# Windowed attention and two MLPs on one core: most raw weight loads issued from GpSimd's DMA queue in place of SyncE's

## The chip, the cores and the metric

The kernel runs on one core of one Trainium2 chip. The metric is the device time of one execution in microseconds (us), the median of several runs. Engines are named as in the profile: PE (TensorE matmuls), PEld (its weight loads), DVE (VectorE), ACT (ScalarE), POOL (GpSimd), SP (SyncE, which here does nothing but issue transfers). A queue of an engine is marked with a q, so SPq is SyncE's instruction queue.

## The reference

Attention over 4 batches and 8 heads of 576 positions with head size 64, where each position sees itself and the 63 before it; its output, 2304 tokens by 512, goes through two MLPs one after the other:

```
scores = q k^T / 8, masked to 0 <= i - j < 64;  attn = softmax(scores) v
h = x @ w_in;   g = s * max(h, 0)^2 + b;                     x = g @ w_out     (layer one, "moe")
h = x @ w_in2;  g = max(h, 0) + alpha * min(h, 0);           out = g @ w_out2  (layer two, "moe2")
```

Each weight matrix is 512 x 2048 or 2048 x 512 in float32; the kernel gets the weights as 64-bit words, 4096 bytes in each of 128 rows for a block of 128 hidden units.

## The kernel before

The hidden dimension of each layer is cut into 16 blocks of 128 units, called f. Layer one takes the blocks in groups of 3, 3, 4, 2 and 4, layer two in four groups of 4. The first two groups of layer one run beside the attention, token block by token block ("the first part of layer one"; up to about 230 us). From then on each group runs over three token spans of 768 in turn. In this second part two blocks f are handled as a pair by a scheme with seven products in place of eight (`hidden_pair`): PE multiplies seven pieces of x with seven pieces of the weights into the tiles `h` and `ab`, ACT copies partial sums between those (line 956), and then both layers' nonlinearity runs on ACT and DVE; `project` multiplies with w_out into `y`. Every float32 operand is split in a high and a low part, and each product is three matmuls.

Weights arrive raw. `converted` makes one step that loads 512 KB of raw words into a tile `raw` (line 640; a ring of three buffers), two ACT steps that read them (lines 644 and 648), and three DVE steps (653/654, 658, 663). After line 663 the raw buffer is free. There are 64 such loads, 32 of w_in and 32 of w_out. The conversion result `wt` is split into high and low parts (lines 670, 672 and 675; 708 and 711 for w_out of layer one). For w_in in the second part, sums of two blocks are formed first, the pieces are written into a staging ring `ag`, stored to HBM (`wd`, line 758) and loaded again from there before they are used (`aw`, line 779). The pieces of x are likewise stored in `xd` (793, 828) and loaded for each span and group (`ax`, line 911). For w_out of layer one, POOL adds the converted block to `wsum` (line 705), from which a bias is made.

All of this is recorded as steps in a `Plan`, and `Plan.emit` writes the instructions out in an order that it finds by list scheduling: each step names the engines that could do it with a cost and a tail after it, a due time `at` and an earliest time `after`. These numbers set only the order in each engine's queue. On the chip each engine takes its queue strictly in order, and waits at an instruction until the semaphores it needs are there. Before the change every transfer stood in SP's queue; POOL's queue held masks, softmax scaling (line 557), sums of x pieces (843) and the `wsum` additions. A raw load is a step for SP at cost `nbytes / 380e3` (1.4) with a tail of 2.0; its due time is that of the conversion less 8, and its earliest time 30 before that.

Of the kernel before, what the change touches and what calls it, by code (L numbers as in the profile page):

```python
# [18 lines left out]
P = 128  # L19
# [18 lines left out]
GRING = 10  # L38
LAG = 1.7
SOON = 16.0  # L40
PAIR_AT = (0, 3584)
W_AT = (0, 1024, 2048, 3584, 4608, 5632)

# [187 lines left out]
def tile_window_attention_two_mlps(  # L231
# [14 lines left out]
    nc = tc.nc  # L246
# [28 lines left out]
    T = Plan()  # L275
# [25 lines left out]
    def act(cols, fn):  # L301
        return ("act", 0.2 + cols * 0.00084, fn, 0.0)

    def dve(cols, fn, fast=False, port=False):
        return ("dve", 0.15 + cols * (0.00053 if fast else 0.00106), fn, 0.0) + (True,) * (fast or port)
# [4 lines left out]
    def dma(n, nbytes, fn):  # L310
        return [("sp", max(n * 0.45, nbytes / 380e3), fn, 2.0)]
# [24 lines left out]
    with tc.manual_schedule():  # L336
# [293 lines left out]
        def converted(layer, f, part, at, after):  # L630

            key = f"w.{layer}.{f}.{part}"
            src = ((w_in1, w_out1), (w_in2, w_out2))[layer][part][f].bitcast(I32)
            raw = T.tile("raw" + key, wst, [P, 512, 2], I32, "raw", 3)
            t = T.tile("t" + key, wst, [P, 512], F32, "wt", 3)
            L = lambda: T[raw][:, :, 0]
            H = lambda: T[raw][:, :, 1]
            ti = lambda: T[t].bitcast(I32)
            T.step(
                dma(1, P * 4096, lambda: nc.sync.dma_start(out=T[raw].rearrange("p a b -> p (a b)"), in_=src)),  # L640
                writes=[(raw, 0), (raw, 1)], at=at - 8, after=after - 8,
            )
            T.step(
                [act(512, lambda: nc.scalar.activation(T[t], H().bitcast(F32), AF.Abs, scale=65536.0))],  # L644
                reads=[(raw, 1)], writes=[t], at=at, after=after,
            )
            T.step(
                [act(512, lambda: nc.scalar.activation(L(), L().bitcast(U32), AF.Copy, scale=2.0 ** -29))],  # L648
                writes=[(raw, 0)], at=at, after=after,
            )  # L650

            def exponent():
                nc.vector.tensor_scalar(T[t], T[t], W_MIN, W_MAX, op0=ALU.max, op1=ALU.min)
                nc.vector.tensor_scalar(ti(), ti(), 3, None, op0=ALU.logical_shift_left)

            T.step([("dve", 0.8, exponent, 0.0, True)], writes=[t], at=at, after=after)
            T.step(
                [dve(512, lambda: nc.vector.scalar_tensor_tensor(  # L658
                    out=L(), in0=H(), scalar=-0x80000000, in1=L(), op0=ALU.bitwise_and, op1=ALU.bitwise_or), port=True)],
                reads=[(raw, 1)], writes=[(raw, 0)], at=at, after=after,  # L660
            )
            T.step(
                [dve(512, lambda: nc.vector.tensor_tensor(ti(), ti(), L(), op=ALU.add), port=True)],  # L663
                reads=[(raw, 0)], writes=[t], at=at, after=after,
            )
            return t
# [20 lines left out]
        def weight(layer, f, part, at, after):  # L687
            t = converted(layer, f, part, at, after)
            key = f"w.{layer}.{f}.{part}"
            slot = (layer * NF + f) % W_SLOTS[part]  # L690
            if part == 0:
                hi = T.place(key + "h", AW, W_AT[slot], 512, F32R)
                lo = T.place(key + "l", AW, W_AT[slot] + 512, 512, F32R)
            else:
                hi = T.tile(key + "h", wts, [P, 512], F32R, f"woh{slot}")
                lo = T.tile(key + "l", wts, [P, 512], F32R, f"wol{slot}")
            if (layer, part) != (0, 1):
                pair(512, lambda: T[t], lambda: T[hi], lambda: T[lo], [t], [key], at, after)
                return

            def total():
                if f == 0:
                    nc.gpsimd.tensor_copy(wsum, T[t])
                else:
                    nc.gpsimd.tensor_add(wsum, wsum, T[t])

            T.step([pool(512, total)], reads=[t], writes=["wsum"], at=at, after=after)
            T.step([act(512, lambda: nc.scalar.activation(T[hi], T[t], AF.Identity, scale=s_sb[:, 0:1]))],
                   reads=[t, "s"], writes=[hi], at=at, after=after)
            T.step(  # L710
                [dve(512, lambda: nc.vector.scalar_tensor_tensor(
                    out=T[lo], in0=T[t], scalar=s_sb[:, 0:1], in1=f32(T[hi]), op0=ALU.mult, op1=ALU.subtract), port=True)],
                reads=[t, hi, "s"], writes=[lo], at=at, after=after,
            )
# [11 lines left out]
        def weight_pair(n, layer, f1, f2, at, after, direct):  # L726


            ts = [converted(layer, f, 0, at, after) for f in (f1, f2)]
            sums_ = T.place(f"s.{n}", AS, 2 * NMAX, 4 * W2)  # L730
            a = lambda i, j: T[ts[i]][:, j * W2:(j + 1) * W2]
# [36 lines left out]
        def w_slot(n, k):  # L768
            lo, hi = PIECES[k]
            return T.place(f"W{k}.{n}", AW, PAIR_AT[n % 2] + 2 * lo * W2, 2 * (hi - lo) * W2, F32R)  # L770

# [98 lines left out]
        def x_pieces(q, at):  # L870


            t1, t2 = 2 * q * HALF, (2 * q + 1) * HALF
            AYv = AY.rearrange("p (k t) -> p k t", k=NK)
            B = lambda r, c: AYv[:, 2 * r:2 * r + 2, (t1, t2)[c]:(t1, t2)[c] + HALF]
            src = lambda r, c: [f"yh{k}.0.{2 * q + c}" for k in (2 * r, 2 * r + 1)]
            temps = {}

            def add(name, a, b, reads):
                t = T.place(f"T{name}.{q}", AS, name % 2 * C, C)  # L880
                temps[name] = t
                T.step(
                    [dve(C, lambda: nc.vector.tensor_sub(x2(T[t]), a(), b()), port=True)], reads=reads, writes=[t], at=at,
                )

            def piece(j, s, reads):
                x_stage(1, q, j, s, reads, at + ORDER.index(j) * PAIR / 7)

            tv = lambda n: (lambda: x2(T[temps[n]]))
            piece(1, lambda: B(0, 0), src(0, 0))  # L890
            add(1, lambda: B(0, 1), lambda: B(0, 0), src(0, 0) + src(0, 1))
            piece(5, tv(1), [temps[1]])
            add(2, lambda: B(1, 1), tv(1), src(1, 1) + [temps[1]])
            piece(6, tv(2), [temps[2]])
            piece(2, lambda: B(1, 0), src(1, 0))
            add(3, lambda: B(1, 1), lambda: B(0, 1), src(1, 1) + src(0, 1))
            piece(7, tv(3), [temps[3]])
            piece(3, lambda: B(1, 1), src(1, 1))
            add(4, lambda: B(1, 0), tv(2), src(1, 0) + [temps[2]])
            piece(4, tv(4), [temps[4]])  # L900
# [16 lines left out]
        def hidden_pair(layer, g, q, p):  # L917
# [5 lines left out]
            if p == 0 and x_load.held != (layer, q):  # L923
                x_load.held = (layer, q)
                if (layer, g) == (1, 0):
                    x_pieces(q, begin[1, 0, q] - SOON)
                for j in ORDER if (layer, g) != (1, 0) else ():
# [290 lines left out]
        for bi in range(NB):  # L1218
            for hp in range(0, NHP, 2 if bi == 0 else 1):
# [7 lines left out]
                before, after = group(hp // 2 if bi == 0 else bi * NHP + hp, bi, (hp, hp + 1) if bi == 0 else (hp,), at1, at2)  # L1227
# [15 lines left out]
        for g in range(SPLIT[0]):  # L1243
            for i, f in enumerate(groups[0][g]):
                for part in range(2):
                    at = FIRST_W[2 * i + part] if g == 0 else begin[0, g, 0] + (i + 2 * part) * pace[g, 0] - 12.0
# [23 lines left out]
        for x, (layer, g) in enumerate(order_of):  # L1270
# [3 lines left out]
            for p in range(len(fs) // 2):  # L1274
                n = number[layer, g, p]
                at = t + p * PAIR
# [5 lines left out]
            for i, f in enumerate(fs):  # L1282
                at = t + LAG * PAIR + i * PAIR / 4 - 12.0 - 15.0 * end
# [77 lines left out]
```

## Time and profile before

| | |
|---|---|
| median of 3 runs | 852.15 us (851.51 to 853.44) |
| profiled execution, own time | 854.11 us |
| its span, first to last instruction | 852.3 us |
| PE busy | 832.7 us (98%) |
| DVE, ACT, POOL busy | 651.1 (76%), 510.5 (60%), 103.5 us (12%) |
| granted TensorE clock, mean | 0.995 |
| DMA | 202.57 MB, mean 238 GB/s |
| raw loads on SPq | 64, of 512 KB |

Busy times add up what an engine did; an instruction that only issues a transfer is not counted. A wait is the idle time just before an instruction, put down to the engine or transfer whose signal came last. "To landing" is the time from the issue of a transfer to its completion signal.

### The profile page before, as it was taken

The page shows a single profiled execution, that of the slowest core. Times are in us where ns is not written, and L with a number is a line of the kernel's source. Part 1 is how long each engine was busy: PE and PEld are TensorE (multiplying, and loading weights), DVE is VectorE, ACT ScalarE, POOL GpSimd, SP SyncE. Part 2 cuts the span into 40 slices and gives each one's busy share as a digit, 9 for nine tenths or more (in the row PEclk, how much of TensorE's full clock was granted, in tenths as well). Part 3 has the DMA queues.
Part 4 walks back from the last instruction along what each step waited for, and adds up shares of the span by engine and source line. Part 5 has one row for each costly group of instructions (what it writes and reads, how often), then busy time and mean ns, then how long its engine had stood idle before and what let it go on. Part 6 is the DMA issues. An engine that isn't in the chain of part 4 may idle for free.

```text
span 852.3 us, 14883 instructions
## 1 busy us (share of the span) xinstructions
PE 832.7 (98%) x5556; PEld 787.7 (92%) x5556; DVE 651.1 (76%) x1175; ACT 510.5 (60%) x1217; POOL 103.5 (12%) x113
## 2 busy tenths in 40 slices
PE   7799999999999999999999999999999999999997
PEld 4678788888899999899999999999999999999997
DVE  6878799797997794699588989867767975864554
ACT  6878997545676474466365667655554754543431
POOL 6543344432100010011000000000000000000000
PEclk9999999999999999999999999999999999999999
DMA  8676973567578979957689359629774769435822
GB/s 282 195 214 179 297 229 111 209 218 275 202 253 316 406 243 363 380 189 305 225 319 340 131 214 354 239 75 346 259 252 156 243 254 348 144 110 187 295 76 75
DMA packets 65592, 202.57 MB, mean 238 GB/s; under 512 B 6640, under 2 KB 25072, under 8 KB 65520
## 3 DMA queue, kind: packets, MB, share of 16 engines
q1 hardware_dynamic: 65520, 201.62, 66.5%
q8 instruction: 44, 0.72, 0.3%
q14 instruction: 28, 0.23, 0.1%
HBM read 143.66 MB, written 57.93 MB: 237 GB/s over the span
## 4 chain that ended last, share of the span: by engine, by line
PE 88%; DMA 5%; ACT 2%; POOL 2%; DVE 1%; issue 1%; SPq 0%; DVEq 0%; POOLq 0%; ACTq 0%
PE y L1158 38%; PE h L945 18%; PE ab L945 13%; PE h L1075 9%; PE y L1135 4%; PE y L605 2%; DMA wd<-ag 2%; DMA raw<-w_out 2%; PE y L574 2%; PE ab L500 1%; DMA raw<-w_in 1%; POOL as__89 L557 1%; ACT as__89 L539 1%; PE ab L1158 0%; PE h L1158 0%
## 5 line engine op out<-in xcount | busy, mean ns | idle before, releaser
L1158 PE MATMUL y<-ax,woh 128*128 128x384 f32 x1216 | 275.4, 334 | 0.4 <-DVE ay L1207 0.4
L1158 PEld LDWEIGHTS y<-ax,woh 128*128 128x128 f32 x1216 | 216.3, 188 | 1.2 <-DVE ay L1207 0.9
L945 PE MATMUL h<-ax,aw 128*128 128x384 f32 x936 | 185.3, 335 | 0.3 <-ACT r L1022 0.2
L1158 PE MATMUL y<-ax,wol 128*128 128x384 f32 x608 | 169.4, 334 | 0.0
L945 PEld LDWEIGHTS h<-ax,aw 128*128 128x128 f32 x936 | 164.2, 188 | 1.4 <-ACT r L1022 0.6
L945 PE MATMUL ab<-ax,aw 128*128 128x384 f32 x702 | 140.4, 335 | 2.0 <-ACT h L956 1.5
L945 PEld LDWEIGHTS ab<-ax,aw 128*128 128x128 f32 x702 | 123.1, 188 | 2.9 <-ACT h L956 1.8
L1158 PEld LDWEIGHTS y<-ax,wol 128*128 128x128 f32 x608 | 111.1, 188 | 0.0
L1015 DVE TENSOR_TENSOR ax<-r,ax 128x384 fp32r<-128x384 f32 x156 | 86.2, 559 | 9.6 <-ACT ax L1010 7.5
L1207 DVE TENSOR_TENSOR ay<-y,ay 128x384 f32<-128x384 f32 x116 | 60.3, 552 | 38.5 <-PE y L1158 38.4
L1075 PE MATMUL h<-ax,aw 128*128 128x512 f32 (+1 forms) x360 | 85.1, 380 | 0.8 <-DVE ax L623 0.6
L1075 PEld LDWEIGHTS h<-ax,aw 128*128 128x128 f32 x360 | 62.8, 192 | 12.9 <-DVE ax L623 1.0
L1045 DVE SCALAR_TENSOR_TENSOR r<-aq,nalpha,r 128x384 f32<-128x384 f32 x96 | 58.5, 613 | 19.6 <-ACT aq L1042 16.6
L644 ACT ACTIVATE wt<-raw 128x512 f32<-128x512 f32 x64 | 43.3, 678 | 37.1 <-DMA raw<-w_out 16.3
L973 DVE TENSOR_TENSOR aq<-ab,aq 128x768 f32<-128x768 f32 x39 | 37.3, 956 | 31.1 <-PE ab L945 29.1
L1010 ACT CAST ax<-r 128x384 fp32r<-128x384 f32 x83 | 42.6, 514 | 25.9 <-DVE r L1045 23.7
L1041 ACT ACTIVATE r<-aq 128x384 f32<-128x384 f32 x48 | 24.8, 517 | 45.8 <-DVE aq L973 45.8
L658 DVE SCALAR_TENSOR_TENSOR raw<-raw 128x512 int32<-128x512 int32 x64 | 47.1, 738 | 1.8 <-ACT raw L648 1.8
L1026 ACT ACTIVATE r<-r 128x384 f32<-128x384 f32 (+2 forms) x90 | 47.5, 542 | 1.1
L557 POOL TENSOR_TENSOR as__89<-as__89,den 128x512 f32<-128x512 f32 x36 | 40.6, 1148 | 56.2 <-DVE den L550 43.7
L648 ACT ACTIVATE raw<-raw 128x512 int32<-128x512 uint32 x64 | 42.9, 679 | 5.7 <-DMA raw<-w_in 4.2
L663 DVE CUSTOM_DVE_ANT_0 wt<-raw,wt 128x1024 uint16<-128x1024 uint16 x64 | 45.0, 706 | 0.5
(140 smaller groups left out, 1149.9 us busy)
## 6 DMA issues: line engine op xcount, KB each, us to landing
ax<-xd SPq DMA_DIRECT2D x91, 768.0 KB, 6.9
wd<-ag SPq DMA_DIRECT2D x33, 512.0 KB, 8.0
aw<-wd SPq DMA_DIRECT2D x33, 512.0 KB, 5.0
raw<-w_in SPq DMA_DIRECT2D x32, 512.0 KB, 5.3
raw<-w_out SPq DMA_DIRECT2D x32, 512.0 KB, 6.4
xd<-ax SPq DMA_DIRECT2D x21, 768.0 KB, 4.3
xd<-aq SPq DMA_DIRECT2D x12, 768.0 KB, 4.1
xd<-ax SPq DMA_DIRECT2D x36, 192.0 KB, 4.6
```

Of the source, the lines that this page charges most:

```text
L557: eng.tensor_mul(x, x, d)
L644: [act(512, lambda: nc.scalar.activation(T[t], H().bitcast(F32), AF.Abs, scale=65536.0))],
L648: [act(512, lambda: nc.scalar.activation(L(), L().bitcast(U32), AF.Copy, scale=2.0 ** -29))],
L658: [dve(512, lambda: nc.vector.scalar_tensor_tensor(out=L(), in0=H(), scalar=-0x80000000, in1=L(), op0=ALU.bitwise_and, op1=ALU.bitwise_or) ...
L663: [dve(512, lambda: nc.vector.tensor_tensor(ti(), ti(), L(), op=ALU.add), port=True)],
L945: nc.tensor.matmul(bank(), W[:, wj, a, kt * P:(kt + 1) * P], X[:, c, kt, :], start=start and kt == 0 and y == 0, stop=kt == 1 and y == 2, ...
L1015: [dve(n, lambda: nc.vector.tensor_sub(T[gl], rn(), f32(T[gh])), port=True)],
L1026: [act(n, lambda: nc.scalar.activation(rn(), rn(), AF.Square)), dve(n, lambda: nc.vector.tensor_mul(rn(), rn(), rn()), port=True)],
L1045: [dve(HALF, lambda: nc.vector.scalar_tensor_tensor(out=rn(), in0=r2n(), scalar=nalpha[:, f:f + 1], in1=rn(), op0=ALU.mult, op1=ALU.add), ...
L1075: nc.tensor.matmul(T[ps][:, :n].rearrange("p (c t) -> p c t", t=P), T[w][:, k * P:(k + 1) * P], T[X(x, k)], start=st, stop=sp,)
L1158: nc.tensor.matmul(ps, T[w][:, m * P:(m + 1) * P], T[x], start=(i == 0 and j == 0), stop=(last and j == 2),)
L1207: ways = [dve(n, lambda a=a, yn=yn: nc.vector.tensor_add(a(), yn(), a()))]
```

## The change

A raw load whose `at` lies above 230 becomes a step for POOL, with a cost of 1.1 and a tail of 4.0, and is issued by GpSimd; the others stay as they were. 47 of the 64 loads move: the 18th and all behind it. Nothing else in the code differs.

```
+OWN_QUEUE = 230.0
...
-            T.step(
-                dma(1, P * 4096, lambda: nc.sync.dma_start(out=T[raw].rearrange("p a b -> p (a b)"), in_=src)),
-                writes=[(raw, 0), (raw, 1)], at=at - 8, after=after - 8,
-            )
+            load = lambda eng: eng.dma_start(out=T[raw].rearrange("p a b -> p (a b)"), in_=src)
+            if at > OWN_QUEUE:
+                ways = [("pool", 1.1, lambda: load(nc.gpsimd), 4.0)]
+            else:
+                ways = dma(1, P * 4096, lambda: load(nc.sync))
+            T.step(ways, writes=[(raw, 0), (raw, 1)], at=at - 8, after=after - 8)
```

The new costs also go into the planner, which orders the other engines a little differently from about 210 us on. On PE the same matmuls stand in nearly the same order; on DVE and ACT seven copies of 1177 and 1075 instructions pass from DVE to ACT. Line numbers after line 38 grow by 1, and after the load by 3 (758 becomes 761, 779 becomes 782, 911 becomes 914, 705 becomes 708).

SP's queue in the middle of the second part of layer one, before (`raw` are raw weights, `ax` pieces of x, `wd` stores of prepared weights, `aw` loads of them):

```order
L640 DMA raw<-w_in 128x1024
L911 DMA ax<-xd 128x1536 x7
L758 DMA wd<-ag 128x1024
L911 DMA ax<-xd 128x1536 x6
L758 DMA wd<-ag 128x512
L758 DMA wd<-ag 128x1024 x2
L640 DMA raw<-w_in 128x1024
L640 DMA raw<-w_out 128x1024 x2
L758 DMA wd<-ag 128x1024
L779 DMA aw<-wd 128x1024 x3
```

The same place of SP's queue with the change:

```order
L761 DMA wd<-ag 128x1024
L914 DMA ax<-xd 128x1536 x5
L761 DMA wd<-ag 128x512
L761 DMA wd<-ag 128x1024
L914 DMA ax<-xd 128x1536 x9
L761 DMA wd<-ag 128x1024 x2
L782 DMA aw<-wd 128x1024 x2
L761 DMA wd<-ag 128x512
```

The three raw loads that stood behind thirteen x loads and four stores have left; the stores still stand behind x loads.

POOL's queue ended before the change with the `wsum` additions, ten in a row:

```order
L843 TENSOR_TENSOR aq<-ax 128x384 x2
L843 TENSOR_TENSOR as__89<-ax 128x384 x4
L705 TENSOR_TENSOR wsum<-wsum,wt 128x512 x10
```

With the change a part of that stretch reads so; behind it come three more additions with two loads between them, and then 26 loads and nothing else:

```order
L640 DMA raw<-w_in 128x1024 x4
L640 DMA raw<-w_out 128x1024 x2
L640 DMA raw<-w_in 128x1024
L708 TENSOR_TENSOR wsum<-wsum,wt 128x512
L640 DMA raw<-w_in 128x1024
L708 TENSOR_TENSOR wsum<-wsum,wt 128x512
L640 DMA raw<-w_in 128x1024 x2
L640 DMA raw<-w_out 128x1024 x2
L708 TENSOR_TENSOR wsum<-wsum,wt 128x512
L640 DMA raw<-w_out 128x1024 x2
```

The loads stand between the additions now; the pairs "w_out x2" and "w_in x2, w_out x2" are, in the list of loads, those that come 27th and 28th and 31st to 34th.

SP's queue in layer two, before, at the place of the 53rd to 55th load:

```order
L911 DMA ax<-xd 128x1536 x6
L758 DMA wd<-ag 128x1024
L758 DMA wd<-ag 128x512
L640 DMA raw<-w_out 128x1024
L779 DMA aw<-wd 128x1024 x2
L640 DMA raw<-w_out 128x1024 x2
L779 DMA aw<-wd 128x1024
```

And with the change:

```order
L914 DMA ax<-xd 128x1536 x5
L761 DMA wd<-ag 128x1024
L914 DMA ax<-xd 128x1536 x2
L761 DMA wd<-ag 128x512
L782 DMA aw<-wd 128x1024 x3
```

The raw loads that stood behind x loads, stores and `aw` loads are gone from it.

## Rows read from the trace of the kernel before

**Rows 1.** Waits of PE from 225 us on: total us, times, longest.
```profile
PE ab L945 <- ACT h L956: 1.5, 1, 1.5
PE ab L945 <- ACT ab L956: 0.5, 1, 0.5
PE y L1158 <- DVE ay L1207: 0.4, 1, 0.4
PE h L945 <- ACT r L1022: 0.2, 1, 0.2
```
**Rows 2.** Chain that ended last, 275 to 400 us: start us, us, what.
```profile
291.30 7.26 DMA raw<-w_out
...
302.13 1.31 PE h L945 x6
...
347.48 11.21 DMA raw<-w_in
...
358.71 0.66 ACT wt L644
...
360.37 1.31 PE ab L945 x6
361.69 1.04 PE h L945 x6
```
**Rows 3.** The same chain, 600 to 660 us.
```profile
622.74 7.19 DMA raw<-w_out
...
634.92 1.33 PE ab L945 x6
```
**Rows 4.** SP's queue in order of time, 268 to 362 us: start, us, line.
```profile
335.37 10.35 SPq L911 DMA_DIRECT2D ax<-xd  x6
...
347.48 0.42 SPq L640 DMA_DIRECT2D raw<-w_in  x1
```
**Rows 5.** Raw loads and last conversion step, start to 273.2 us: ns min/median/max, first and last start.
```profile
L640 SPq DMA_DIRECT2D raw<-w_in x16: 327/423/897, 1.6 to 268.2; - x16
...
L640 SPq DMA_DIRECT2D raw<-w_out x10: 327/340/446, 7.4 to 227.6; - x10
...
L663 DVE CUSTOM_DVE_ANT_0 wt<-raw,wt x24: 676/684/1495, 11.2 to 272.3; 128x1024 uint16<-128x1024 uint16 x24
```
**Rows 6.** The same, start to 347.4 us.
```profile
L640 SPq DMA_DIRECT2D raw<-w_in x19: 327/422/897, 1.6 to 317.1; - x19
...
L640 SPq DMA_DIRECT2D raw<-w_out x12: 327/386/496, 7.4 to 297.8; - x12
...
L663 DVE CUSTOM_DVE_ANT_0 wt<-raw,wt x31: 676/685/1495, 11.2 to 330.4; 128x1024 uint16<-128x1024 uint16 x31
```
**Rows 7.** The same, start to 614.9 us.
```profile
L640 SPq DMA_DIRECT2D raw<-w_in x28: 327/373/897, 1.6 to 585.0; - x28
L640 SPq DMA_DIRECT2D raw<-w_out x24: 327/426/1355, 7.4 to 536.0; - x24
...
L663 DVE CUSTOM_DVE_ANT_0 wt<-raw,wt x52: 676/685/1495, 11.2 to 597.5; 128x1024 uint16<-128x1024 uint16 x52
```
**Rows 8.** ACT's waits for raw loads in line 644 from 225 us on.
```profile
ACT wt L644 <- DMA raw<-w_out: 16.3, 10, 3.6
...
ACT wt L644 <- DMA raw<-w_in: 9.8, 4, 4.8
```
**Rows 9.** ACT in order of time, 353 to 362 us.
```profile
358.71 0.66 ACT L644 ACTIVATE wt<-raw 128x512 f32<-128x512 f32 x1 [3.38 <-DMA raw<-w_in]
```
**Rows 10.** All raw loads (line 640): issue to landing.
```profile
DMA to landing us min/median/max: 3.3/5.6/12.7
```
**Rows 11.** POOL's additions of line 705, whole span: ns min/median/max, first and last start.
```profile
L705 POOL TENSOR_TENSOR wsum<-wsum,wt x15: 1281/1301/1881, 31.2 to 389.4; 128x512 f32<-128x512 f32 x15
```
**Rows 12.** DVE's line 658, whole span.
```profile
L658 DVE SCALAR_TENSOR_TENSOR raw<-raw x64: 642/686/1532, 9.2 to 736.7; 128x512 int32<-128x512 int32 x64
```
**Rows 13.** Busy time by stretch: PE, PEld, DVE, ACT, POOL, clock, DMA share, GB/s.
```profile
325.00:350.00 25.00, 24.62 (x142) 24.30 (x141) 13.89 (x29) 11.94 (x25) 0.00 (x0) 1.00 0.98 362
```

## The prediction, made before the changed kernel ran

> **What bounds the kernel now.** I read first how long PE waits, and for whom. From 225 us on it waits four times in some 620 us, 1.5 + 0.5 + 0.4 + 0.2 = 2.6 us in all [rows 1]; the rest of that time it multiplies, so nothing but these waits can be won there. The change moves nothing before about 210 us. Next I read the chain that ended last around each wait. Three of the four lead back through ACT to a raw load that landed late: the loads of 291.30, 347.48 and 622.74 us take 7 to 11 us, and PE resumes at 302.13, 360.37 and 634.92 [rows 2, 3]. These are the waits of 0.2, 1.5 and 0.5 us. Nobody on PE reads raw words. What PE lacks are ACT's copies and activations of partial sums, which stand in ACT's queue behind a conversion that waits for its load: ACT stood idle for 3.38 us until the load of 347.48 had landed, and the next thing that it does is the copy for PE [rows 9, 2]. From 225 us on ACT waits so in 14 conversions, for 26.1 us together [rows 8]; most of it PE doesn't feel, because it works off sums that it already has.
>
> So the question is why these loads came late. The buffers were not the reason. By 347.4 us 19 + 12 = 31 loads had been issued, and 31 conversions had ended with line 663, the last begun at 330.4 [rows 6]: from 331 us all three buffers lay empty, and the next load left at 347.48. SP's queue shows what it did meanwhile: six x loads took it from 335.37 to 345.7, since each waits until PE has done with the piece that it overwrites, and the raw load stood behind them [rows 4]. At 614.9 us it is 52 loads and 52 conversions, the last begun at 597.5 [rows 7], so three empty buffers from 598.2 on, and the load of the chain left at 622.74. At 273.2 us it is 26 loads and 24 conversions [rows 5]: one buffer of three was empty from 273.0, and the load left at 291.30, 18 us later.
>
> **What the change removes.** The three loads of the chain stand in POOL's queue now. Ahead of them there are other raw loads, which need buffers that free up in the same order, and additions to `wsum`, which need conversions that have ended by then. So each can go when its buffer is empty: 18.3, 16.5 and 24.5 us sooner (291.30 - 273.0, 347.48 - 331.0, 622.74 - 598.2). To be harmless they have to land before ACT asks: that was at 358.71 - 3.38 = 355.3 for the second [rows 9], and about 295 for the first, if the longest wait for a w_out, 3.6 us, is its own [rows 8].
>
> What a load from POOL takes, no row shows, since no transfer left POOL before. From below I bound it by SP's loads, 3.3 us to landing at the least [rows 10]. From above I take the longest landing of any raw load, 12.7 us [rows 10], and the longest addition that could occupy POOL just ahead, 1.9 us [rows 11]: 14.6 us. Also with the upper end the loads land at 287.6, 345.6 and 612.8 us, before ACT asks. I take a value near the median, 5.6 us, and about 1 us more, an estimate from POOL's addition of 1.3 us, the nearest thing that it does with a tile of this width. The three waits go: 0.2 + 1.5 + 0.5 = 2.2 us.
>
> A wait costs more than its idle time. The six matmuls behind each of the three take 1.31, 1.31 and 1.33 us, six others 1.04 [rows 2, 3], so each restart costs some 0.28 us: 0.8 us for three. Together 3.0 us.
>
> **What it adds.** POOL gets 47 issues. From 225 us on it had nothing but ten additions, and each addition waits for DVE anyway; a delay of one holds only the bias, much later. POOL and DVE do slow each other: an addition takes 1.28 to 1.88 us, and line 658 on DVE 0.64, but 1.53 at worst [rows 11, 12]. If an issue costs DVE as much as an addition can, 0.9 us, at 47 places, that is 42 us over 500 us on an engine that is busy 13.89 of 25 us in the stretch around the largest wait [rows 13]. One such delay is smaller than the ACT wait of 3.38 us, of which PE felt 1.5, so I count nothing for it; without that cover it would be at most 0.9 us a time. The seven copies that pass from DVE to ACT I count as nothing for the same reason.
>
> Of the 47 loads many were issued before, too, as soon as a buffer was empty: the fourth of a run needs the buffer of the first. They win nothing and pay the longer way. But the planner now counts 1.1 + 4.0 = 5.1 us from issue to use where it counted 3.4, so that it puts such a conversion 1.7 us later in ACT's queue; the extra 1 us is covered.
>
> What stays is the wait of 0.4 us behind DVE's `ay`, and what comes next: the stores to `wd` still stand behind x loads in SP's queue, and ACT and DVE wait for the staging ring. For one new wait of this kind I set 0.5 us, the second largest of the four, an estimate.
>
> Sum for the profiled execution: 854.11 - 3.0 + 0.5 = 851.6 us. It lies 1.96 us above the median of the runs, 852.15, so the forecast for the median is 852.15 - 2.5, rounded to 849.6 us.
>
> **A rule against it.** The raw transfers share their engines with all others: in the stretch of the largest wait the DMA share is 0.98 [rows 13], and a load that leaves sooner is not moved for free. The Trainium skill ("DMA: Bandwidth & Descriptors", section "Issuing engines are not separate DMA queues") says that transfers of all issuing engines run on the same 16 engines, so that spreading them saves only the issue time; by that rule the sum would be about nothing. The rows show a third thing, waiting in line: 10 us in which SP stands at x loads with three raw buffers empty [rows 4, 6]. I go by them.
>
> The same skill ("SBUF — State Buffer", section "SBUF: two separate sides") warns that GpSimd writes its transfers' descriptors through a port that DVE can lock, and gives 3100 ns in place of 620 for such a transfer. By that figure a load would take 2.5 us more, an estimate that no row here can test; the three loads have more than that in hand, but it would bring the slower rival below nearer, without reaching the 4 us from which that one decides.
>
> **The rivals.**
> - Gained and given back. With the raw loads gone, another wait in ACT's or DVE's queue (the staging ring, or an x piece that shares the DMA engines with a raw load that now comes sooner) takes their place. For it: the fourth wait is of that kind, and the windows at a DMA share near 1. Against it: PE never waited for an `ax` or `aw` load [rows 1]. Two such waits of 1 us with their restarts give back 2.6 us: 851.8.
> - Nothing is moved. If bandwidth alone made the three landings late, the loads would be as late from any queue: 852.1. Against it: the issue itself came 16 to 24 us after the buffer was empty.
> - Slower. The fourth loads of the runs come late, because a load through POOL takes far longer: DVE holds POOL up each time. ACT can wait about 3.38 - 1.5 = 1.9 us before PE feels it [rows 9, 1], and the planner's 1.7 us come on top, so PE stops when a load takes over 3.6 us more than SP's. In the second part there are some ten runs with a fourth load; at 4.1 us more, ten times 0.5 us and as many restarts of 0.28 make 7.8 us, less the 3.0 won: 857. From 4 us on it decides. Against it: the nearest rows, the stretched addition (0.6 us) and the stretched DVE operation (0.9) [rows 11, 12], are far below.
>
> **How the numbers follow.** Forecast 0.55; given back 0.20; nothing moved 0.10; slower 0.15. A measurement of this kernel can tell some 0.2%, 1.7 us: below 850.4 counts as faster, above 853.9 as slower. The forecast reaches from 848.4 (all four waits and restarts gone, 2.6 + 4 x 0.28 = 3.7) to 850.4; of "given back" a quarter still lies below 850.4. So faster 0.60, the same 0.27, slower 0.13 (the mildest of the slow cases stay within 0.2%). For the range I take off the lower end the 0.6 us by which the fastest run lies under the median: 847.8; the upper end goes to 853.2, the two middle rivals and half of the runs' upper spread of 1.3 us, and leaves out most of the slow case and little else, some 0.17.
>
> **What would show it.** In the profile of the changed kernel there should be a second DMA queue with 47 x 512 KB = 24.6 MB; the chain should hold no raw load at 291, 347 and 622 us; ACT's waits for raw loads should fall from 26.1 to below 8 us; PE's waits from 225 us on should come to 1 us or less. POOL's loads should leave within 2 us of the end of a conversion. The prediction is wrong if raw loads from POOL take over 9 us in the median, or if PE waits for an operation that stands behind a `wd` store or an `ax` load.

## The result, and the profile of the changed kernel

| | before | changed |
|---|---|---|
| median of 6 runs | 853.57 us (851.51 to 853.85) | 865.25 us (862.21 to 866.91) |
| ratio | | 1.0138 [1.0115, 1.0162] |
| profiled execution, own time / span | 854.11 / 852.3 us | 866.68 / 864.9 us |
| PE busy / not busy in the span | 832.7 / 19.6 us | 837.1 / 27.8 us |

It became 1.4% slower, where 0.3% faster was forecast. The forecast of 849.6 us, its range and its sign were all wrong. The span grew by 12.6 us: 8.2 us in which PE stood still and 4.4 us in which it was busy for longer with the same matmuls. Not all of that is the change's. The clock granted in the first 55 us was 0.88 in this execution and 0.94 in the one before, and at 200 us, where the first moved load leaves, PE is 1.8 us behind with the same work (its 1901st weight load starts at 203.41 in place of 201.60). The kernel with only the later loads moved, which is the kernel before up to 388 us, shows 0.97 there, so this differs from execution to execution. The times of the two traces are to be compared with these 1.8 us in mind.

The page of the changed kernel: busy time, and the two DMA queues that carry data (packets, MB, share of 16 engines).

```profile
PE 837.1 (97%) x5552; PEld 791.3 (91%) x5556; DVE 650.2 (75%) x1168; ACT 515.4 (60%) x1224; POOL 128.6 (15%) x160
...
q1 hardware_dynamic: 58752, 176.98, 57.4%
q0 software_dynamic: 6768, 24.64, 8.1%
```

The loads did move: q0 is new, and 24.64 MB are 47 loads of 512 KB. PE's waits from 225 us on, which answer to [rows 1] (the lines are three higher in the changed kernel: 945 is 948, 1158 is 1161, 670 is 673):

```profile
PE y L1161 <- DVE ay L1210: 5.8, 2, 4.7
PE h L948 <- ACT h L959: 1.6, 1, 1.6
PE ab L948 <- ACT h L959: 1.5, 2, 1.2
PE h L948 <- DMA ax<-xd: 1.1, 1, 1.1
PE y L1161 <- DVE ax L1018: 0.5, 1, 0.5
```

They sum to 10.5 us, where they were 2.6: 7.9 of the 8.2 us that PE stood still for longer. The wait of 1.5 us at 360 and that of 0.5 at 635 are gone, but new ones stand in their place, one of them of 4.7 us, which ends at 301.50. The chain that ended last leads to it (start us, us, what):

```profile
272.68 7.11 DMA raw<-w_in
...
285.32 14.15 DMA wd<-ag
...
299.55 0.16 ACT ag L673
...
300.07 0.53 ACT r L1029
...
300.62 0.36 DVE ax L1014
300.98 0.48 DVE ay L1210
...
301.50 1.33 PE y L1161 x3
302.83 1.92 PE ab L948 x6
```

Read it backwards from PE. `project` needs DVE's `ay`; that stands on DVE behind an `ax` that needs ACT's `r`; that stands on ACT behind the write of a piece into the staging ring `ag`; and the ring is full until a store to `wd` has landed, 14.15 us after it was issued. The six matmuls of `ab` just behind took 1.92 us instead of 1.04. The same happens once more in layer two: the chain there holds a store issued at 595.12 that took 12.71 us, and PE waits 1.6 us at 605.48 and 1.2 us at 610.07 behind ACT's waits for the ring. ACT's waits from 225 us on show the exchange (total us, times, longest), the changed kernel first, then two lines of the kernel before:

```profile
ACT ag L673 <- DMA wd<-ag: 12.5, 6, 5.8
...
ACT raw L651 <- DMA raw<-w_in: 7.7, 4, 3.9
...
ACT wt L647 <- DMA raw<-w_in: 2.8, 3, 1.4
...
ACT raw L651 <- DMA raw<-w_out: 2.7, 1, 2.7
...
ACT wt L647 <- DMA raw<-w_out: 1.6, 2, 1.4
```

```profile
ACT ag L670 <- DMA wd<-ag: 5.9, 4, 3.2
ACT raw L648 <- DMA raw<-w_in: 4.2, 3, 2.2
```

Waits for raw loads fell to 14.8 us; counted in the same way they were 30.3 before, the 26.1 of [rows 8] and 4.2 more in line 648. ACT's waits for the staging ring rose from 5.9 to 12.5 us (DVE's fell from 5.1 to 2.9). The stretch around the long wait, put together from the trace's issue and landing times of single transfers (queue, start, landing, us):

```
before                                    changed
SP   wd<-ag     282.19 289.96   7.8       POOL raw<-w_out 275.46 283.97   8.5
SP   wd<-ag     282.66 291.71   9.1       SP   wd<-ag     282.31 291.01   8.7
SP   wd<-ag     283.13 292.93   9.8       SP   wd<-ag     285.32 299.47  14.2
SP   wd<-ag     285.95 294.15   8.2       POOL raw<-w_out 286.15 295.71   9.6
SP   raw<-w_out 291.30 298.56   7.3       POOL raw<-w_in  289.27 298.55   9.3
```

Before, the load of 291.30, which the prediction called late, left 5 us after the last of these four stores. In the changed kernel a load goes ahead of the stores and two more run beside the one that ACT needs. Two x loads, issued at 283.86 and 284.91 just ahead of that store, took 10.2 and 13.0 us, so the raw loads weren't all that ran beside it. The DMA share from 285 to 300 us was 1.00 before and is 1.01 now: the engines had nothing to spare in either kernel.

### The profile page after: what moved, and what is told of

Its sections match the earlier page's. It is cut to its first block, busy times and chain, and to the rows that moved or that the text cites. A ratio compares the mean times of both kernels' runs of the same rounds, so it can differ in the third digit from the quotient of the medians.

```text
span 864.9 us, 14920 instructions
## 1 busy us (share of the span) xinstructions
PE 837.1 (97%) x5552; PEld 791.3 (91%) x5556; DVE 650.2 (75%) x1168; ACT 515.4 (60%) x1224; POOL 128.6 (15%) x160
## 3 DMA queue, kind: packets, MB, share of 16 engines
q0 software_dynamic: 6768, 24.64, 8.1%
## 4 chain that ended last, share of the span: by engine, by line
PE 76%; DMA 11%; DVE 7%; ACT 3%; issue 2%; POOL 1%; DVEq 0%; POOLq 0%; ACTq 0%
PE y L1161 32%; PE h L948 15%; PE ab L948 12%; PE h L1078 5%; PE y L1138 4%; DMA wd<-ag 4%; DMA xd<-aq 3%; PE y L606 2%; DMA raw<-w_in 2%; PE y L575 2%; PE ab L501 2%; DMA raw<-w_out 1%; DMA ax<-xd 1%; POOL as__89 L558 1%; ACT as__89 L540 1%
## 5 line engine op out<-in xcount | busy, mean ns | idle before, releaser
L1018 DVE TENSOR_TENSOR ax<-r,ax 128x384 fp32r<-128x384 f32 x156 | 86.1, 559 | 14.1 <-ACT ax L1013 12.5
L640 POOL DMA_DIRECT2D raw<-w_out x25 | 14.0, 561 | 290.5 <-DVE wt L666 69.7
```

What stands on the lines that cost most here:

```text
L1018: [dve(n, lambda: nc.vector.tensor_sub(T[gl], rn(), f32(T[gh])), port=True)],
```

## The experiments

Each was timed in rounds beside the kernel before; ratios are to its median on the same chip (853.27 us for the first four kernels, 852.35 for the next four, 852.91 for the last four, in the order of their numbers). Two parts of the change are told apart first. One is the queue: which engine issues the loads. The other is the order: the planner, told that a load is a step for POOL with other numbers, writes out other queues on all engines.

**The queue alone** (`e1_queue_only`). The planner gets the numbers of before, so that PE, DVE and ACT have exactly the rows of before; only the issuing engine changes.

```
+            load = lambda eng: eng.dma_start(out=T[raw].rearrange("p a b -> p (a b)"), in_=src)
+            eng = nc.gpsimd if at > OWN_QUEUE else nc.sync
+            ways = dma(1, P * 4096, lambda: load(eng))
+            T.step(ways, writes=[(raw, 0), (raw, 1)], at=at - 8, after=after - 8)
```

> The same 47 loads leave from GpSimd's queue, but the planner counts them as before, so that PE, DVE and ACT keep the order of the kernel before, row for row, and POOL's queue reads as in the changed kernel. If the new queue is the cause (raw loads leave as soon as a buffer is empty and share the DMA engines with the stores to wd, which then land late), this is slow too: 860 to 868 us, with a long PE wait behind a wd store. If the planner's new order is the cause, this shows the gain that was forecast: 849 to 852 us.

Measured: 855.74 us, 1.0027 [1.0010, 1.0044]. Its PE waits from 225 us on and two rows of its chain:

```profile
PE ab L946 <- ACT h L957: 1.4, 1, 1.4
PE y L1159 <- DVE ay L1208: 1.3, 1, 1.3
PE ab L946 <- ACT ab L957: 0.4, 1, 0.4
PE h L946 <- ACT r L1023: 0.3, 1, 0.3
...
284.56 12.17 DMA wd<-ag
...
298.82 1.33 PE ab L946 x6
```

The same store is late here, 12.17 us, with not one instruction of PE, DVE or ACT in another place. So the queue by itself makes the wait at 299, and the change loses a little even without the planner. The waits of 360 and 635 us are gone, as forecast; the four that are there come to 3.4 us, 0.8 more than before. The medians differ by 2.5 us (855.74 - 853.27), and this one profile doesn't show where the rest goes.

**The order alone** (`e2_order_only`). The change's numbers for the planner, and SP still issues.

```
-                ways = [("pool", 1.1, lambda: load(nc.gpsimd), 4.0)]
+                ways = [("pool", 1.1, lambda: load(nc.sync), 4.0)]
```

> The planner counts the loads as in the changed kernel (1.1 and 4.0, on POOL), so that PE, DVE and ACT have the changed kernel's order, row for row, but the loads leave from SP's queue. If the new queue is the cause: 852 to 856 us. If the order is the cause: 860 to 868 us.

Measured: 859.75 us, 1.0072 [1.0050, 1.0094]. PE waits, and its chain at the second wait of 4.3:

```profile
PE y L1161 <- DVE ay L1210: 4.3, 2, 2.7
PE ab L948 <- ACT h L959: 1.5, 1, 1.5
...
352.41 0.33 SPq L914
...
352.79 11.28 DMA wd<-ag
...
366.84 2.20 PE y L1161 x6
```

Half of the loss comes with no load on POOL at all. Here a store stood behind an x load and then took 11.28 us. The first wait, of 2.7 us at 298.00, has the cause of the changed kernel's: in the new order the 27th and 28th raw load leave at 282.67 and 284.05, from SP's own queue, ahead of a store issued at 284.61, which took 11.4 us. Before they left behind the stores, at 291.30 and 297.79. So at this place the order sends the raw loads early by itself, without GpSimd's queue.

**Only the later loads** (`e3_queue_late`): as the queue alone, with 26 loads from GpSimd instead of 47.

```
-OWN_QUEUE = 230.0
+OWN_QUEUE = 430.0
```

> As the first kernel of this set, with the bound at 430 in place of 230: only the 26 loads from about 390 us on leave from GpSimd's queue, where POOL has nothing else to do. If the new queue is the cause, the waits near 300 and 350 us go and only those from 600 us on stay: 853 to 857 us. If the order is the cause: 850 to 853 us.

Measured: 851.59 us, 0.9982 [0.9965, 1.0000]. The first of these loads leaves at 388.08 us. PE waits 1.3 us in all, 0.8 at 340 and 0.5 at 358, and not once after 390. By the medians these loads alone gain 853.27 - 851.59 = 1.7 us, with an interval that reaches 1.0000; the prediction's sum has 0.8 us for that part, the wait of 0.5 and its restart. Up to 388 us this kernel is the one before, instruction for instruction, and yet its wait near 358 us is 0.5 us where it was 1.5. So a wait in a single profile can differ by 1 us between executions of the same work, and small differences of waits prove little.

**A longer staging ring** (`e4_staging`): the change, with 512 more elements per partition for `ag`. Between 3 and 23 rows of an engine's order differ from the changed kernel's.

```
-    AG = area("ag", 2 * GH * NMAX)
+    AG = area("ag", 2 * GH * NMAX + 512)
```

> The changed kernel with a staging ring of 4608 columns in place of 4096, so that the first piece of a pair has a place of its own and need not wait for the store of the pair before; the order of all engines is nearly that of the changed kernel (3 to 23 rows differ). If the time is lost where ACT waits for a wd store before it may write the ring, the wait near 300 us shrinks: 855 to 860 us. If it is lost elsewhere (order, x loads): 863 to 867 us.

Measured: 860.09 us, 1.0084 [1.0055, 1.0114]. About 0.5% comes back, though the wait of 299 us is still there with 3.5 us. The ring is probably part of the loss, and this much more of it isn't enough; the rows that moved with it were not tried apart.

**Four loads, given back and alone** (`e5_keep4`, `e6_only4`). The queue alone, without four loads that come around the late store; and only these four (the 27th, 28th and the next two of w_in). In the queue alone they leave at 274.82, 285.33, 288.61 and 306.92: one ahead of the stores of 283 to 288 us, two beside them and one behind.

```
+            eng = nc.gpsimd if at > OWN_QUEUE and not 320 < at < 333 else nc.sync
```

```
+            eng = nc.gpsimd if 320 < at < 333 else nc.sync
```

> The order of the kernel before and GpSimd's queue as in the first experiment, except that four loads stay in SP's queue: w_out 10 and 11 of layer one and w_in 0 and 1 of layer two (due times 321.9 to 332.7), the ones that left between 275 and 289 us just ahead of the stores to wd. If those four take the DMA engines away from the stores, PE's waits of 0.4 and 1.4 us at 294 and 299 us go and the time falls by about 2 us against the first experiment, to 852 to 854 us; the loads of 347 and 622 us still come early. If the loads from GpSimd slow the kernel in a general way (DVE, its port, the longer path), it stays at 855 to 856 us.

> The reverse: only these four loads leave from GpSimd's queue, all others from SP's, in the order of the kernel before. If the collision with the stores is the cause of the loss, the waits near 294 and 299 us are there and the wait at 302 us is gone: 853 to 856 us, not below the kernel before. If raw loads that leave early are harmless: 851 to 853 us.

Measured: 853.43 us, 1.0010 [0.9996, 1.0024], without the four; 856.99 us, 1.0054 [1.0036, 1.0071], with only the four. ACT's wait for the staging ring without the four and, in the second fence, with only them, and that kernel's chain:

```profile
ACT ag L671 <- DMA wd<-ag: 3.2, 2, 2.0
```

```profile
ACT ag L671 <- DMA wd<-ag: 7.9, 4, 5.1
...
281.58 12.03 DMA wd<-ag
...
295.71 1.33 PE ab L946 x6
```

These four alone make the store late and cost no less than the whole queue. Without them the late store at that place is gone, and with it PE's waits of 294 and 299 us; the time is that of the kernel before. The times carry this reading, and the waits only in part: with only the four, PE's new waits there are 1.0 and 0.7 us, where the median grew by 4.6 us (856.99 - 852.35), and the profiled execution, 854.44 us, is one of that kernel's fastest. Without the four PE still waits 4.1 us in all, at other places.

**The stores instead of the loads** (`e7_store_queue`): the kernel before, with the stores to `wd` issued by GpSimd and every raw load left on SP.

```
-                    dma(1, P * cols * 8, lambda: nc.sync.dma_start(out=wd[n, :, 2 * lo * W2:2 * hi * W2], in_=f32(T[t]))),
+                    dma(1, P * cols * 8, lambda: nc.gpsimd.dma_start(out=wd[n, :, 2 * lo * W2:2 * hi * W2], in_=f32(T[t]))),
```

> The kernel before in its own order, with the raw loads in SP's queue, and the 44 stores to wd issued from GpSimd's queue instead. If what counts is that stores get to the DMA engines ahead of x loads and raw loads, the wait at 341 us (DVE behind a store) goes and the landings of the stores fall from 8 to about 6 us: 849 to 853 us. If only the raw loads' lateness counts, nothing changes: 852 to 854 us.

Measured: 849.58 us, 0.9966 [0.9949, 0.9983]. From 225 us on no PE wait is left in the view. ACT's waits, the stores' row of the DMA view (KB each, median us to landing), and ACT's conversion of the 32nd load in order of time:

```profile
ACT wt L644 <- DMA raw<-w_out: 16.5, 12, 3.7
ACT wt L644 <- DMA raw<-w_in: 4.4, 4, 1.7
...
ACT ag L670 <- DMA wd<-ag: 0.5, 1, 0.5
...
wd<-ag POOLq DMA_DIRECT2D x33, 512.0 KB, 6.8
...
354.74 0.68 ACT L644 ACTIVATE wt<-raw 128x512 f32<-128x512 f32 x1 [0.88 <-DMA raw<-w_in]
```

ACT's wait for the ring fell from 5.9 to 0.5 us and DVE's from 5.1 to none in the view. ACT's waits for raw loads fell less, from 30.3 to some 25 us, but where PE felt them most they went as well: the 32nd load, that of 347.48 before [rows 2], no longer stands behind stores in SP's queue. It left at 344.34 and landed at 354.71, and ACT waited 0.9 us for it in place of 3.4 [rows 9]. Before, PE's wait of 0.4 us at 341 came behind a store, and its largest, 1.5 us at 360, behind this load. So moving the stores helped both kinds of transfer, and the run doesn't tell how much each gave.

**What in the planner's numbers does it** (`e8_engine_only`, `e12_tail_only`). SP issues in both. One changes only the engine the planner counts the loads on, with the cost and tail of before; the other only the time from issue to use, to the 5.1 us of the change.

```
+                ways = [("pool", P * 4096 / 380e3, lambda: load(nc.sync), 2.0)]
```

```
+                ways = [("sp", P * 4096 / 380e3, lambda: load(nc.sync), 3.7)]
```

> The loads leave from SP's queue, and the planner counts them on POOL, but with SP's cost and tail (1.4 and 2.0), so that another order of all engines comes out. If it is the length 1.1 + 4.0 that makes the order bad, this is near the kernel before: 851 to 855 us. If it is that SP looks free of them in the plan, so that its queue is laid out with x loads ahead of stores and raw loads meeting both on the chip, it is as slow as the second experiment: 857 to 862 us.

> The loads in SP's queue and planned on SP at their old cost of 1.4, with a tail of 3.7 in place of 2.0 (5.1 us from issue to use, as in the changed kernel): another order again. If it is the plan's belief that SP is free of raw loads that spoils the order, this one is near the kernel before: 850 to 855 us. If any new order does it, the kernel before being a lucky one: 856 to 862 us.

Measured: 858.50 us, 1.0079 [1.0064, 1.0094], for the engine; 851.94 us, 0.9988 [0.9969, 1.0006], for the tail. The tail costs nothing, though it too makes another order, in which six copies pass from DVE to ACT (DVE has 1169 instructions and ACT 1223). So not every new order costs time, and some copies more on ACT need not. The engine costs as much as the whole order, in an order of its own with fifteen such copies. That a planner which counts the loads on POOL takes SP to be free is how the code works; that this is what spoils the order is argued from single places. The chain of the engine's kernel shows one, a raw load that left behind an x load:

```profile
316.57 0.32 SPq L914
...
316.94 0.47 SPq L640
...
317.47 7.88 DMA raw<-w_out
...
326.66 0.56 DVE ay L1210
...
327.26 3.08 PE y L1161 x12
```

**Stores moved too** (`e9_order_store`: the order alone; `e10_after_store`: the whole change; `e11_late_store`: the later loads). All with the stores' edit of above added.

> The changed kernel's order on PE, DVE and ACT, row for row, raw loads in SP's queue (as in the second experiment, 859.75 us), and the stores to wd from GpSimd's queue. If the new order costs time because it leaves stores behind x loads in SP's queue, the waits at 298 and 366 us behind a wd store go, and with them most of the 6 us: 850 to 854 us. If the order is bad for PE, DVE and ACT themselves, it stays at 857 to 861 us.

> The changed kernel, with the stores to wd issued from GpSimd's queue too, behind raw loads that wait there for a buffer. If stores that land late are what the changed kernel loses by, it gains most of its 12 us back: 852 to 857 us. If raw loads that wait in the same queue hold the stores up, or the early raw loads still take the DMA engines from them, 858 us or more.

> The order of the kernel before, stores to wd from GpSimd's queue, and the 26 raw loads from about 390 us on from GpSimd's queue too: the two changes that were faster, together. The stores alone left PE almost no wait after 225 us (0.9 us of lost starts), so there is nothing for the loads to win: 848 to 851 us, the same as the stores alone. If the two are in each other's way in one queue, 851 us or more.

Measured: 856.38 us, 1.0039 [1.0021, 1.0057]; 862.05 us, 1.0113 [1.0089, 1.0138]; 849.12 us, 0.9957 [0.9946, 0.9969]. Moving the stores gives 0.33% with the order alone (1.0039 / 1.0072) and 0.25% with the whole change or the later loads, about as by itself (0.34%): so the order costs 0.7% whether the stores stand in SP's or in POOL's queue, and their place in SP's queue isn't the whole of it. In the second kernel the stores share POOL's queue with the loads, and the late one stood behind them (its chain):

```profile
283.85 0.53 POOL raw L640
...
284.46 11.44 DMA wd<-ag
```

The third has the lowest median of all kernels here, 0.43% below the one before; from moving the stores alone (0.9966) it can't be told apart.

## Why the prediction was wrong

**What was right.** Three raw loads waited in SP's queue with empty buffers [rows 4, 6, 7]. From GpSimd these three left 0.7 us after the conversion that freed their buffer, and 43 of the 47 within 2 us, as forecast; three of the other four stood behind an addition to `wsum` that waited 17.5 us for DVE. With the queue alone PE's waits of 360 and 635 us were gone. The issue and landing of the moved loads (line 640 of the changed kernel: ns min, median, max; then us to landing):

```profile
L640 POOL DMA_DIRECT2D raw<-w_out x25: 527/530/802, 199.6 to 722.8; - x25
L640 POOL DMA_DIRECT2D raw<-w_in x22: 527/530/570, 237.2 to 677.0; - x22
...
DMA to landing us min/median/max: 3.7/5.2/13.4
```

That is 5.2 us in the median over all 64, 47 of them from POOL, where it was 5.6 [rows 10], and the upper bound of 14.6 us held. The later loads alone gave 0.18% [0.00, 0.35].

**The step that failed first: "What it adds", the one new wait of 0.5 us.** The mechanism was named there and in the rival "Gained and given back", which was priced at two waits of 1 us. It is one of 4.7 us and six of 0.3 to 1.6, 10.5 us in all, of which 7.5 are those at 301.50, 605.48 and 610.07 behind the ring. Two things made it too small. I priced it by PE's smallest waits [rows 1], not by what a store loses when a raw load runs beside it: 14.2 us to landing, where the neighbours of before took 7.8 to 9.8. And I took it as evidence that PE had never waited for an `ax` load [rows 1]; that row was measured in the order and the traffic of before. The changed kernel has such a wait, 1.1 us for an x load at 407.61. It comes with the order: the queue alone has none, the order alone one of 0.2 us, and two of 0.5 with the stores moved. The four-load runs bear this step out for the queue's part: the four loads alone 1.0054, all without them 1.0010.

**The step that failed next: the planner.** The prediction counted the longer path, 1.7 us later in ACT's queue, and called it covered. That was right, the tail alone is 0.9988 [0.9969, 1.0006]. It also called the seven copies that pass from DVE to ACT nothing, which the tail's six bear out in part, and did not price what the planner does when it counts the loads on POOL and no longer on SP. This is 1.0079 [1.0064, 1.0094] alone, more than half of the loss. Which of the moved rows does it stays open: with the stores out of SP's queue 3.3 us of PE waits are left in the order alone, in eight places, most of it for ACT's copies (1.8 us) and x loads (1.0).

**The sum.** 0.27% of the queue and 0.72% of the order are 0.99%, the change is 1.38%. The rest of 0.39% is hardly more than the intervals allow (half-widths of 0.17, 0.22 and 0.24). Where both meet, at 301.50, the store lands at 299.47; with the queue alone it was 296.73, with the order alone 295.97. That the two add up on the same store is read from the traces, not tried apart. One sum of the prediction doesn't come out: the upper end of its range, 853.2, should be 852.8 by its own working (852.1 and half of 1.3), which changes nothing here.

**The restart.** 0.28 us each holds for the waits up to 1.6 us in the changed kernel: 1.33 us for the six matmuls of `ab` or `h` behind them. Behind the wait of 4.7 us, 15 matmuls took 4.60 us; at 1.04 us for six they take 2.6, so 2.0 less. That is nearly half of the 4.4 us by which PE was busy for longer, of which another 1.0 lies in the first 200 us; the prediction had no term for it.

**The rule against it.** The prediction went by the wait in line and against the Trainium skill ("DMA: Bandwidth & Descriptors", section "Issuing engines are not separate DMA queues"). For the raw loads the runs side with the rule and go further: their gain came out of the stores and x loads, whose medians to landing went from 8.0 to 8.7 and from 6.9 to 7.2 us (8.4 and 7.1 with the queue alone, 7.9 and 6.9 with the order alone). The rule isn't the whole: moving the stores to another issuing engine gained 0.34%, and a raw load that had stood behind them left 3.1 us sooner.

**The rivals.** "Nothing is moved" is out: the raw loads left early, and ACT waited half as long for them. "Slower" had the right sign by another mechanism: the path through POOL is not longer. The Trainium skill's 3100 ns for a transfer that DVE holds up ("SBUF — State Buffer", section "SBUF: two separate sides") is not seen in these rows: POOL's issues took 527 to 802 ns beside a DVE that was busy for 465.82 of the last 640 us. Whether DVE just then ran an operation that locks the port, no row shows. One piece of that rival did come: a fourth load left when its buffer came free, at 344.20, took 8.35 us, and PE waited 1.2 us for the copy behind it at 353.66.

Of what was to show it, the second queue, the loads' leaving within 2 us (but for four) and their median below 9 us came true; ACT's waits for raw loads came to 4.4 us in the line of [rows 8], but to 14.8 with the line behind it. PE's waits did not (10.5 us in place of 1), and raw loads still stand in the chain, at 260.25, 272.68 and 344.20, though not at the three places named. The last sign of a wrong prediction, PE behind a `wd` store or an `ax` load, came at 301.50, 407.61, 605.48 and 610.07.

## What to carry to other kernels

A transfer that stands in line with empty buffers may be what keeps the DMA engines free for another: before moving it, list what lands in the same stretch and who waits for that, and where the DMA share is near 1 try first to move the transfer that somebody waits for (here the stores) and not the bulk that can wait. Where a planner writes the order, an edit of one step's engine is two edits: make the queue and the order in separate kernels, since the order alone was the larger part here. A row that shows no wait for a transfer says so only for the traffic that it was measured in.

## What the runs showed of the hardware that was not expected

Behind some waits PE ran at half its clock for a while. Windows of the changed kernel (columns as in [rows 13]) before, in and behind the slow matmuls:

```profile
296.50:301.50 5.00, 0.34 (x2) 0.02 (x1) 0.88 (x3) 1.95 (x5) 0.00 (x0) 0.75 1.02 413
301.50:306.10 4.60, 4.60 (x15) 4.60 (x16) 3.19 (x6) 2.02 (x5) 0.00 (x0) 0.53 0.42 127
306.10:311.00 4.90, 4.90 (x30) 4.90 (x29) 4.83 (x10) 3.57 (x9) 1.97 (x2) 1.00 0.72 252
```

A granted clock of 0.53 over the stretch is 1.2 GHz for nearly all of it, and 2.4 GHz behind it. The order alone shows it twice, behind a wait of 2.7 us and behind one of 1.56:

```profile
298.00:302.40 4.40, 4.40 (x16) 4.40 (x17) 3.50 (x7) 2.38 (x6) 0.00 (x0) 0.61 0.86 287
...
366.84:370.70 3.86, 3.86 (x13) 3.86 (x14) 3.14 (x7) 0.00 (x0) 0.00 (x0) 0.56 0.56 228
```

The kernel with only the planner's engine changed shows both outcomes: 0.65 behind a wait of 2.4 us, and full clock behind one of 2.5 us:

```profile
327.26:332.20 4.94, 4.93 (x19) 4.94 (x20) 3.10 (x6) 1.85 (x4) 0.00 (x0) 0.65 1.00 418
...
357.16:362.00 4.84, 4.84 (x27) 4.77 (x28) 4.48 (x10) 3.16 (x7) 0.00 (x0) 1.00 0.79 312
```

So the length of the last wait alone doesn't decide, and what does stays open here. Where it comes, it costs 1.6 to 2.0 us (13 matmuls in 3.86 us and 15 in 4.60, each less 0.173 a matmul), as much as a short wait itself.
